# Later post-mixes, conversions moved between stages, q loaded once, other relayouts at the start of a fused attention and expert kernel

## The chip, the cores and the metric

The kernel runs on one core of a Trainium2 chip. The metric is device time in microseconds (us) of one execution. Before the change three runs took 1535.59, 1542.51 and 1545.74 us, median 1542.51. The profile is of a further execution, which took 1539.95 us.

## The reference

Three layers follow each other, in float32 (the weights of the last layer come as float64 and are converted on the chip):

```python
# attention with head mixing before and after the softmax: batch 4, heads 12, seq 448, head_dim 64
scores = scale * q @ k.T                                # per batch and head
scores = einsum('bhij,hg->bgij', scores, w_pre)         # "pre-mix" over the heads
attn   = exp(scores - max) / (sum + 1e-9)
attn   = einsum('bhij,hg->bgij', attn, w_post)          # "post-mix"
x      = (attn @ v) as [1792 tokens, 768]
# experts: 8 of them, each token goes to one (argmax of x @ w_gate), 768 -> 1024 -> 768
y[mask] = gate * (relu(x[mask] @ w1[e]) @ w2[e])
# last layer for all tokens: 768 -> 2048 -> 768
h = relu(y @ w_in); out = (h * h) @ w_out
```

## The kernel before, in words

**Prologue and attention (to about 650 us).** Each batch's 448 query rows are cut into four chunks (120, 110, 120, 98 rows; 16 chunks), and each chunk into groups of 10 rows, 180 groups in all. For a chunk, `qk` makes the scores of a head for all its rows on TensorE, ScalarE puts them into `raw`, and SP stores two heads at a time in a DRAM scratch `scr`. For a group, `pump` loads a tile `r` whose partitions are (row, head), so that `premix` is one matrix product with a block-diagonal matrix. `rmax` and `exp` give the tile `e` and its row sums; `wscale` makes their reciprocals on VectorE for two groups, `wmul` scales the post-mix matrix on GpSimd (`wr`), `postmix` multiplies `e` with `wr`, `a_hi` and `a_lo` split the result in two parts (a rounded part and the rest, as all operands of the products in float32r are split), and `av` multiplies two chunks at a time (a pair, 23 or 22 groups) with v.

The order is written out by hand. A loop runs over slots `t` from -10 to the end; slot `t` holds the pre-mix of group `t`, and a dictionary `plan` says in which slot `postmix`, `av`, `xout`, `qk`, `q_load`, `q_trans`, the loads and splits of k and v go. `LAG` is the number of slots by which the post-mixes follow the pre-mixes (from the second pair on; `L0` is that of the first pair); the last `AVS` slots of a pair hold `av` and no post-mix. All engines and DMA queues take their instructions in the order in which they are issued here, and an instruction that waits holds back those behind it on its engine.

The first chunk is special. Its q and all k of the first batch are loaded whole into `qa` and `ka`, its scores stay in SBUF as `raw0`, and its first three groups are relayouted straight from `raw0` (rows `g0` to `g0+10`, which are ten neighbouring partitions), the others through `scr`. q lies twice side by side (`z` in 0, 1), by two loads. `warm` issues products on zeros, whose results are not used.

`tick` is called three times in a slot. It hands out steps of the router (which sorts tokens to experts) and of `convert`: `w_in` and `w_out` come as float64 and each half (128 rows x 384 columns) is turned into float32 by seven VectorE steps (`Conv.parts`, lines 916 to 924) and stored in DRAM (`wi`, `wo`). Of 64 halves, 36 are converted during the attention.

**Experts (to about 1045 us).** `Moe.run` walks through units of 128 tokens, in pairs of a double unit (two units together, `double1`, `double2`) and a single one (`stage1`, `stage2`). Weights stream in, and every tile is split by ScalarE (line 1044) and VectorE or GpSimd (line 1045). The remaining 28 halves of `w_out` are converted here: after each step of a double unit (from the second one on) `CD` says how many conversion steps follow on VectorE.

**Last layer (to the end).** For four blocks of tokens and 16 slices of the 2048 columns: `st1` (line 1266), `relu2` (1276 to 1279), `st2` (1296, 1298). The converted weights are loaded from `wi` and `wo` and split again (`split_in`, `split_out`; the latter's rest is formed on GpSimd).

## Time and profile before

| what | value |
|---|---|
| median of three runs | 1542.51 us (1535.59 to 1545.74) |
| the profiled execution | 1539.95 us, its span 1538.2 us |
| TensorE (PE) busy | 1407.9 us, 92% of the span |
| TensorE weight loads (PEld) busy | 1203.7 us, 78% |
| VectorE (DVE) busy | 1035.6 us, 67% |
| ScalarE (ACT) busy | 825.1 us, 54% |
| GpSimd (POOL) busy | 466.3 us, 30% |
| moved by DMA | 279.25 MB, mean 182 GB/s |

An engine's busy time is the sum of the spans of its instructions; waiting doesn't count. Matrix products are pipelined and their ends are modelled, so a busy TensorE isn't a TensorE at its peak. The granted clock (PEclk) is a share of full speed. The name to the right of an arrow in a wait is the instruction that ended it.

### The profile page before, as it was taken

The page shows a single profiled execution, that of the slowest core. Times are in us where ns is not written, and L with a number is a line of the kernel's source. Part 1 is how long each engine was busy: PE and PEld are TensorE (multiplying, and loading weights), DVE is VectorE, ACT ScalarE, POOL GpSimd, SP SyncE. Part 2 cuts the span into 40 slices and gives each one's busy share as a digit, 9 for nine tenths or more (in the row PEclk, how much of TensorE's full clock was granted, in tenths as well). Part 3 has the DMA queues.
Part 4 walks back from the last instruction along what each step waited for, and adds up shares of the span by engine and source line. Part 5 has one row for each costly group of instructions (what it writes and reads, how often), then busy time and mean ns, then how long its engine had stood idle before and what let it go on. Part 6 is the DMA issues. An engine that isn't in the chain of part 4 may idle for free.

```text
span 1538.2 us, 25510 instructions
## 1 busy us (share of the span) xinstructions
PE 1407.9 (92%) x8541; PEld 1203.7 (78%) x8541; DVE 1035.6 (67%) x2331; ACT 825.1 (54%) x1677; POOL 466.3 (30%) x567
## 2 busy tenths in 40 slices
PE   8579998999899999889788889999999999999996
PEld 6367876787687778789677888897888888888896
DVE  3488888888988887689789889767233332422373
ACT  3357775777687767635355455564234332433453
POOL 2034232423342332233233322223222322312253
PEclk6799999999999999999899999999999999999998
DMA  7788778877877674247988988755323423433361
GB/s 145 192 237 232 221 211 246 222 207 210 242 224 219 202 208 137 99 141 189 237 245 230 290 277 300 251 180 174 103 93 90 145 85 103 128 99 97 99 196 54
DMA packets 174459, 279.25 MB, mean 182 GB/s; under 512 B 63919, under 2 KB 119535, under 8 KB 174319
## 3 DMA queue, kind: packets, MB, share of 16 engines
q1 hardware_dynamic: 166459, 254.67, 57.3%
q10 hardware_dynamic: 4788, 10.26, 2.3%
q0 software_dynamic: 3072, 12.59, 2.3%
q8 instruction: 70, 1.15, 0.3%
q14 instruction: 70, 0.57, 0.1%
HBM read 219.60 MB, written 63.51 MB: 184 GB/s over the span
## 4 chain that ended last, share of the span: by engine, by line
PE 45%; DVE 17%; DMA 4%; issue 3%; ACT 1%; POOL 0%; DVEq 0%; SPq 0%; POOLq 0%; ACTq 0%
PE ps L1266 15%; PE psb L1296 10%; PE po L1298 4%; DVE w1l L1045 3%; DVE w2l L1045 2%; PE x L270 2%; PE psb L1124 2%; PE a L236 2%; PE s L190 2%; DMA craw<-in_moe_w_out_dram 2%; DMA r<-in_moe_w_dram 2%; PE psa L1093 1%; PE qk L165 1%; DVE sm L199 1%; DVE atl L255 1%
## 5 line engine op out<-in xcount | busy, mean ns | idle before, releaser
L1045 POOL TENSOR_TENSOR w2l<-r,w2h 128x768 fp32r<-128x768 f32 x88 | 171.0, 1944 | 465.5 <-ACT w2h L1044 449.3
L1277 DVE TENSOR_TENSOR room<-room 128x512 f32<-128x512 f32 (+1 forms) x64 | 56.5, 883 | 233.3 <-ACT room L1276 233.3
L236 PE MATMUL a<-wr,e 120*128 120x120 f32 (+1 forms) x1440 | 190.8, 280 | 24.0 <-POOL wr L227 23.2
L236 PEld LDWEIGHTS a<-wr,e 120*128 120x128 f32 (+1 forms) x1440 | 180.8, 195 | 37.1 <-POOL wr L227 29.2
L165 PE MATMUL qk<-kt,qt 128*120 128x448 f32 (+2 forms) x384 | 175.0, 541 | 20.2 <-DVE qt L107 18.4
L1266 PE MATMUL ps<-yb,w1h 128*128 128x512 f32 (+1 forms) x640 | 181.7, 369 | 0.9 <-DVE yb L1253 0.5
L190 PE MATMUL s<-r,wprebd 120*120 120x448 f32 x360 | 172.4, 561 | 9.0 <-DMA r<-scr 4.5
L1296 PE MATMUL psb<-w2h,h 128*128 128x512 f32 x448 | 170.3, 396 | 0.0
L1044 ACT CAST w2h<-r 128x768 fp32r<-128x768 f32 x160 | 132.6, 834 | 65.4 <-PE psb L1124 28.2
L1044 ACT CAST w1h<-r 128x1024 fp32r<-128x1024 f32 (+1 forms) x136 | 128.3, 947 | 70.8 <-DMA r<-in_moe_w_dram 20.9
L1276 ACT ACTIVATE room<-ps 128x512 f32<-128x512 f32 (+1 forms) x64 | 34.9, 545 | 227.7 <-PE ps L1266 227.5
L1045 DVE TENSOR_TENSOR w1l<-r,w1h 128x768 fp32r<-128x768 f32 (+1 forms) x124 | 139.1, 1133 | 25.8 <-ACT w1h L1044 23.6
L227 POOL TENSOR_SCALAR wr<-wpostbd,sm 120x120 f32<-120x120 f32 x180 | 103.8, 587 | 159.8 <-DVE sm L215 80.8
L205 ACT ACTIVATE e<-s,sm 120x448 f32<-120x448 f32 x180 | 115.0, 639 | 56.5 <-DVE sm L199 55.9
L165 PEld LDWEIGHTS qk<-kt,qt 128*120 128x120 f32 (+2 forms) x384 | 70.0, 190 | 89.1 <-issue 48.9
L199 DVE TENSOR_REDUCE sm<-s 120x1 f32<-120x448 f32 x180 | 112.4, 624 | 36.0 <-PE s L190 31.4
L250 ACT CAST ath<-a 128x480 fp32r<-128x480 f32 x180 | 101.7, 568 | 64.0 <-PE a L236 63.1
L1266 PEld LDWEIGHTS ps<-yb,w1h 128*128 128x128 f32 x640 | 111.7, 189 | 22.8 <-DVE yb L1254 1.5
L166 ACT COPY raw<-qk 120x448 f32<-120x448 f32 (+2 forms) x186 | 97.9, 531 | 41.4 <-PE qk L165 29.2
L1266 PE MATMUL ps<-yb,w1l 128*128 128x512 f32 (+1 forms) x320 | 118.2, 369 | 0.8 <-DVE w1l L1045 0.8
L1124 PE MATMUL psb<-h,w2h 128*128 128x256 f32 x576 | 111.5, 295 | 0.0
L1093 PE MATMUL psa<-room,w1h 128*128 128x256 f32 x576 | 107.4, 288 | 0.0
(321 smaller groups left out, 3241.0 us busy)
## 6 DMA issues: line engine op xcount, KB each, us to landing
r<-in_moe_w_dram SPq DMA_DIRECT2D x72, 512.0 KB
r<-in_moe_w_dram SPq DMA_DIRECT2D x96, 384.0 KB
r<-scr SPq DMA_DIRECT2D x173, 210.0 KB
r<-wi SPq DMA_DIRECT2D x64, 384.0 KB
r<-wo SPq DMA_DIRECT2D x64, 384.0 KB
scr<-raw SPq DMA_DIRECT2D x48, 420.0 KB
craw<-in_moe_w_in_dram SPq DMA_DIRECT2D x32, 384.0 KB
craw<-in_moe_w_out_dram ACTq DMA_DIRECT2D x26, 384.0 KB
```

The costliest lines, as they stand in the source:

```text
L165: nc.tensor.matmul(ps[0:n], lhsT=qts[C, h // 2][:, z, h % 2, 0:n], rhs=kts[b, h], start=z == 0, stop=z == 1)
L190: nc.tensor.matmul(ps[0:m], lhsT=const["wpre"][0:m, 0:m], rhs=rts.pop(G)[0:m], start=True, stop=True)
L199: nc.vector.reduce_max(sms[G // 2][0:m, o:o + 1], pss[G][0:m], axis=AX.X, negate=True)
L205: nc.scalar.activation(t[0:m], pss.pop(G)[0:m], AF.Exp, bias=sm[0:m, o:o + 1], accum_out=sm[0:m, 2 + o:3 + o])
L227: nc.gpsimd.tensor_scalar(w.rearrange("p (g i) -> p g i", i=gm), src, sm[0:m, 6 + o:7 + o], None, ALU.mult)
L236: nc.tensor.matmul(o, lhsT=e[0:m, JT[jc]:JT[jc] + JP], rhs=w, start=True, stop=True)
L1044: nc.scalar.copy(hi, raw)
L1045: (nc.gpsimd if on_pool else nc.vector).tensor_tensor(out=lo, in0=raw, in1=hi, op=ALU.subtract)
L1093: self.nc.tensor.matmul(o, lhsT=w[:, ms], rhs=x, start=k == 0 and j == 0 and m % 2 == 0, stop=k == K1 - 1 and j == 2, skip_group_check=True)
L1124: self.nc.tensor.matmul(o, lhsT=w[:, ms], rhs=x, start=k == 0 and j == 0 and m % 2 == 0, stop=k == K2 - 1 and j == 2, skip_group_check=True)
L1266: self.nc.tensor.matmul(ps[:, 0:n], lhsT=w[:, ks], rhs=x[:, 0:n], start=k == 0 and m == 0, stop=k == KD - 1 and m == 2)
L1296: self.nc.tensor.matmul(main, lhsT=x[:, ts], rhs=w[:, 0:512], start=f == 0 and m == 0, stop=f == NF - 1 and m == 2)
```

## The change

What it does, part by part:

- Post-mixes, `av` and `xout` come one slot later (`LAG` 8 to 9), with one more buffer for `e` and one less for `r`; each `wmul` is issued at the earliest three slots ahead of its post-mix instead of with its `wscale`.
- The attention converts only `w_in` (32 halves), from the 13th slot on. The experts' stage converts 18 halves of `w_out`, two or one steps at a time instead of four to two. The other 14 are converted in the first block of the last layer, in place (`conv_out`).
- q is loaded once; for the first chunk by the ACT queue and doubled by ScalarE, for the others by SP and doubled by GpSimd (`q_copy`). The loads of the constants come behind, on the ACT queue.
- The first chunk's rows lie so that the first five groups take every fifth partition of 50, and all five are relayouted straight from `raw0`; `scr` gets the rows from 50 on only.
- The loads of v of the first batch come four slots later and its splits five; three warming products follow each of the first four heads of the prologue.

```diff
-    WARM, WARM2, RB = 12, 6, 6
+    WARM, WARM2, RB = 12, 6, 5
     Q1 = {4: (0, 4), 6: (4, 8), 8: (8, 12)}
...
     r_p = pool("r", RB)
-    e_p = pool("e", 8)
+    e_p = pool("e", 9)
     wr_p = pool("wr", 6)
...
         b, i0, m = chunks[C]
-        for z in range(2):
-            nc.sync.dma_start(a[0:m, :, z], q[b, h:h + n, i0:i0 + m, :].rearrange("h p d -> p h d"))
+        src = q[b, h:h + n, i0:i0 + m, :].rearrange("h p d -> p h d")
+        k = 0 if C else RB * GI
+        for g in range(0 if C else RB):
+            nc.scalar.dma_start(a[g:k:RB, :, 0], src[g * GI:(g + 1) * GI])
+        (nc.sync if C else nc.scalar).dma_start(a[k:m, :, 0], src[k:m])
+        copies.append((a, m))
+    copies = []
+    def q_copy():
+        a, m = copies.pop(0)
+        nc.gpsimd.tensor_copy(a[0:m, :, 1], a[0:m, :, 0])
...
         if h % 2 == 1:
-            nc.sync.dma_start(scr[C][0:n, h - 1:h + 1, :], raws[C][0:n])
+            k = 0 if C else GI * RB
+            nc.sync.dma_start(scr[C][k:n, h - 1:h + 1, :], raws[C][k:n])
...
         pend.extend(range(first[C], first[C + 1]))
-        pump(RB if C else 3)
+        pump()
...
             t = r_p.tile([GP, S], F32, tag="r", name="r")
-            if G < 3:
-                nc.sync.dma_start(t[0:m * H], raw0[g0:g0 + m])
+            if G < RB:
+                nc.sync.dma_start(t[0:m * H], raw0[G:GI * RB:RB])
             else:
...
         sm, o = sms[G // 2], G % 2
-        if o == 1:
-            sms.pop(G // 2)
         w = wr_p.tile([GP, H, GI], F32, tag="wr", name="wr")
...
-    plan = {}
+    plan, scale = {}, {}
...
     AVS, LEAD, L0 = 5, 4, 4
-    LAG = AVS + 3
+    LAG = AVS + 4
     for P in range(len(pairs)):
...
             g = LAG if P else L0
-            at(f + g + s * (w + LAG - g) // n, postmix, f + s)
+            t = f + g + s * (w + LAG - g) // n
+            at(t, postmix, f + s)
+            scale.setdefault(max((f + s) // 2 * 2 + 3, t - 3), []).append(f + s)
         for z in range(6):
...
         if g % 2 == 0:
-            at(3 * g // 2, v_load, 0, g)
-        at(3 * g // 2 + 2, v_split, 0, g)
+            at(3 * g // 2 + 4, v_load, 0, g)
+        at(3 * g // 2 + 7, v_split, 0, g)
     for C in range(NC_):
...
                     at(f + u * n // 6 - 8, q_load, C + 1, u)
+                if u % 2 == 0:
+                    at(f + u * n // 6 - 3, q_copy)
                 at(f + u * n // 6 - 2, q_trans, C + 1, u)
...
-    q_all(0, 0, 4)
+    q_all(0, 0, H)
     k_all(0, 2)
     k_all(2, 6)
-    q_all(0, 4, H)
     k_all(6, H)
...
         kns[0, h] = ka[:, h]
+    nc.scalar.copy(qa[0][:, :, 1], qa[0][:, :, 0])
+    copies.clear()
     warm(WARM)
...
             q_all(1, *Q1[h])
+        if h < AH + 2:
+            warm(3)
     fill_const(0)
...
             wscale((t - 3) // 2)
-            wmul(t - 3)
-            wmul(t - 2)
+        for G in scale.get(t, ()):
+            wmul(G)
         tick(ps_q, 0, busy, t - NG)
...
 CR = 3
-NP = 18
-FF = 1024
+FF, F2 = 1024, 2048
+K1, K2, NF = KD, FF // 128, F2 // 128
 TS = 2
...
 XK = ((4,6),(3,5))
-CD = (4,4,4,4,4,4),(4,4,4,4,3,2,2,2)
+CD = (2,2,2,2,2,2),(2,2,2,2,2,2,1,1)
 PH = (3,4,5,6,7,8,9,9,10,12,13)
...
 ZS = (12,14,16,18,20,22)
-F2 = 2048
-K1, K2, NF = KD, FF // 128, F2 // 128
 PE, END = "PE", "END"
...
         self.ph, self.py = {}, {}
-        self.todo = [(g >= NF, g % NF, z) for g in range(NP, 2 * NF) for z in range(2)] if self.main else []
+        self.todo = [(1, f, z) for f in range(NF) for z in range(2) if z == 0 or f < 2] if self.main else []
         self.loads = list(self.todo)
...
         for kind, f, z in self.todo:
-            if z == 0:
-                cw = self.cw_p.tile([128, DM], F32, tag="cw", name="cw")
             a = self.cv_p.tile([128, 384], I32, tag="ca", name="ca")
             r = self.cv_p.tile([128, 384], F32, tag="cr", name="cr")
-            yield from cv.parts((kind, f, z), cw[:, z * 384:(z + 1) * 384], a, r)
+            cw = self.cw_p.tile([128, 384], F32, tag="cw", name="cw")
+            yield from cv.parts((kind, f, z), cw, a, r)
             self.conv_load(self.nc.scalar)
-            if z == 1:
-                self.nc.sync.dma_start(cv.wo[f * 128:(f + 1) * 128] if kind else cv.wi[f], cw)
+            self.nc.sync.dma_start(cv.wo[f * 128:(f + 1) * 128, z * 384:(z + 1) * 384], cw)
...
         f = self.seq[i][1]
-        self.nc.sync.dma_start(self.raw2[i % K2], self.cv.wo[f * 128:(f + 1) * 128, :])
+        n = 384 if self.main and 2 <= i < NF else DM
+        self.nc.sync.dma_start(self.raw2[i % K2][:, 0:n], self.cv.wo[f * 128:(f + 1) * 128, 0:n])
+    def conv_out(self, i):
+        cv = self.cv
+        a, r = self.froom("h").bitcast(I32)[:, 0:384], self.froom("l")[:, 0:384]
+        out = self.raw2[i % K2][:, 384:DM]
+        for _ in cv.parts((1, i, 1), out, a, r):
+            yield
+        self.nc.sync.dma_start(cv.wo[i * 128:(i + 1) * 128, 384:DM], out)
+        if i + 4 < NF:
+            self.conv_out_load(i + 4)
+    def conv_out_load(self, i):
+        self.cv.load((1, i, 1), self.raw1[2 + i % 4][:, 0:DM].bitcast(I32), self.nc.sync)
...
-    def relu2(self, i):
+    def relu2(self, i, conv):
         nc = self.nc
...
         nc.vector.tensor_tensor(out=g[:, 0:n], in0=g[:, 0:n], in1=g[:, 0:n], op=ALU.mult)
+        next(conv, None)
         nc.scalar.copy(hi[:, 0:n], g[:, 0:n])
...
                     assert False
+            conv = self.conv_out(i + 2) if main and i + 2 < NF else iter(())
             if i < N:
-                self.relu2(i)
+                self.relu2(i, conv)
+            for _ in conv:
+                pass
             if i < N and self.seq[i][1] == NF - 1 and self.seq[i][0] + 1 < len(blocks):
...
         self.yb_p = self.pool("yb", 1)
+        if self.main:
+            for i in range(2, 6):
+                self.conv_out_load(i)
...
             const = emit_ident(tc, c0, c1)
-            load_consts(tc, c1, const, w_pre, w_post, w_gate)
             cx_p = c1.enter_context(tc.tile_pool(name="cx", bufs=2))
...
-                keys = [(g >= NF, g % NF, z) for g in range(NP) for z in range(2)]
+                keys = [(0, f, z) for f in range(NF) for z in range(2)]
...
                 for i, key in enumerate(keys):
-                    kind, f, z = key
+                    _, f, z = key
                     a, r = [xs_p.tile([128, DM // 2], F32, tag=f"c{n}", name="cx") for n in range(2)]
...
                             zs = slice(z * 384, (z + 1) * 384)
-                            nc.sync.dma_start((cv.wo[f * 128:(f + 1) * 128] if kind else cv.wi[f])[:, zs], r)
+                            nc.sync.dma_start(cv.wi[f, :, zs], r)
                             load(i + 2)
...
                     steps[:] = route(new), None
-                    next(conv)
                 if last:
                     cur[1] += 1
-                    for _ in range(1 if busy and cur[1] % 2 else 2):
+                    for _ in range(0 if cur[1] < 13 else 2 if cur[1] % 3 == 0 or not busy else 1):
                         next(conv, None)
...
                 if part:
+                    load_consts(tc, c1, const, w_pre, w_post, w_gate)
                     rt.fill()
```

## Rows read from the trace of the kernel before

**Rows 1.** Busy us (count) by stretch: PE, PEld, DVE, ACT, POOL, PEclk, DMA, GB/s.

```profile
10.00:34.00 24.00, 24.00 (x79) 20.09 (x78) 10.95 (x29) 9.82 (x21) 5.08 (x13) 0.50 0.69 154
...
34.00:51.00 17.00, 0.93 (x4) 0.31 (x2) 3.46 (x9) 0.34 (x1) 0.00 (x0) 0.60 0.45 110
...
60.00:110.00 50.00, 37.55 (x188) 27.69 (x187) 35.63 (x98) 26.42 (x65) 15.23 (x24) 0.86 0.86 239
...
110.00:600.00 490.00, 459.75 (x2930) 373.53 (x2929) 412.88 (x1238) 363.31 (x939) 170.45 (x268) 0.99 0.76 216
...
704.00:977.00 273.00, 233.01 (x1615) 217.09 (x1614) 244.10 (x367) 138.23 (x179) 85.35 (x68) 0.94 0.86 252
...
1054.00:1187.00 133.00, 132.78 (x657) 110.96 (x657) 44.75 (x63) 45.60 (x70) 28.14 (x15) 0.99 0.33 95
```

**Rows 2.** Timeline of the prologue: start us, us, engine, line, operation, out<-in, count.

```profile
0.83 1.40 ACTq L455 DMA_DIRECT2D wprerep<-in_w_pre_dram  x1
...
2.18 4.79 PE L350 MATMUL warm<-wz 120*120 120x448 f32 x12 [2.18 <-DVE wz L345]
...
3.08 0.50 ACTq L457 DMA_DIRECT2D idwg<-in_moe_w_gate_dram  x1
...
7.21 0.36 ACT L98 CAST qt<-qtp 128x240 fp32r<-128x240 f32 x1 [2.31 <-PE qtp L96]
...
17.53 1.10 PE L165 MATMUL qk<-kt,qt 128*120 128x448 f32 x2
...
21.77 1.10 PE L165 MATMUL qk<-kt,qt 128*120 128x448 f32 x2
```

**Rows 3.** Timeline behind the prologue; in brackets the idle time before, and its releaser.

```profile
32.82 4.34 SPq L182 DMA_DIRECT2D r<-raw  x3
...
37.21 3.12 SPq L170 DMA_DIRECT2D scr<-raw  x1
...
40.38 2.50 SPq L904 DMA_DIRECT2D craw<-in_moe_w_in_dram  x2
...
47.36 0.36 DVE L916 TENSOR_SCALAR cx<-craw 128x384 int32<-128x384 int32 x1 [13.40 <-DMA craw<-in_moe_w_in_dram]
...
51.17 0.71 PE L165 MATMUL qk<-kt,qt 128*110 128x448 f32 x1 [15.81 <-DVE qt L107]
...
54.70 0.92 PE L190 MATMUL s<-r,wprebd 120*120 120x448 f32 x2
...
64.74 1.82 PE L190 MATMUL s<-r,wprebd 120*120 120x448 f32 x2 [4.51 <-DMA r<-scr]
```

**Rows 4.** TensorE's waits, 60 to 600 us: us in total, times, longest.

```profile
PE a L236 <- POOL wr L227: 20.9, 19, 3.5
```

**Rows 5.** TensorE's waits, 75 to 110 us.

```profile
PE a L236 <- POOL wr L227: 7.2, 3, 3.5
```

**Rows 6.** VectorE's groups, 704 to 977 us: count, busy us, mean ns, idle before.

```profile
L917 DVE SCALAR_TENSOR_TENSOR ca<-craw,ca 128x384 int32<-128x384 int32 x28 | 20.0, 713 | 0.6
...
L916 DVE TENSOR_SCALAR ca<-craw 128x384 int32<-128x384 int32 x28 | 16.1, 576 | 13.8 <-DMA craw<-in_moe_w_out_dram 13.8
...
L918 DVE TENSOR_SCALAR craw<-craw 128x384 int32<-128x384 int32 x28 | 13.1, 469 | 0.8
```

**Rows 7.** TensorE's timeline where the second double unit starts.

```profile
704.14 0.40 PE L1093 MATMUL psa<-room,w1h 128*128 128x256 f32 x2
```

**Rows 8.** Chain that ended last, from 976 us: start us, us, what.

```profile
976.89 9.86 PE psa L1093 x72
...
1023.63 8.19 PE psa L1152 x36
...
1031.82 4.23 PE psa L1184 x24
```

**Rows 9.** The same chain in the last layer.

```profile
1076.15 4.18 PE ps L1266 x18
...
1084.57 4.18 PE ps L1266 x18
```

## Prediction

> **What bounds the kernel now.** I read the busy time by stage first [rows 1], then the stretches whose TensorE share is low, in order of time, and last what TensorE waited for. Four things are to be seen. From 10 to 34 us TensorE is recorded busy all the time, but at a granted clock of 0.50. From 34 to 51 us it is idle but for 0.93 us. In the attention (110 to 600 us) it is busy 459.75 of 490 us, so at most 30 us are to be had there. In the first expert stage (704 to 977 us) it is busy 233 of 273 us while VectorE is busy 244 and the DMA engines 0.86, so VectorE and the transfers set that stage. In the last stage (1054 us on) TensorE is busy 132.78 of 133 us and VectorE only 44.75: nothing is to be gained there, and VectorE has room.
>
> **The dead stretch after the prologue.** TensorE waits 15.81 us for `qt` from VectorE [rows 3]. VectorE does nothing either: its next instruction in order is the first conversion step, which waits 13.40 us for `craw`, and `q_lo`, which makes `qt`, is queued behind it. `craw` is late because SP first issues three `r<-raw` (4.34 us) and the last `scr<-raw` (3.12 us) and gets to `craw` at 40.38. The change starts no conversion before the 13th slot, so this wait is gone. Late next is the transfer for the first pre-mix. TensorE stood still from 51.17 - 15.81 = 35.4 us, and from its restart to the first pre-mix it needed 54.70 - 51.17 = 3.5 us: ready at 38.9. The five direct relayouts begin on SP where the three did, at 32.8; at a third of 4.34, 1.45 us, for each, the first is issued by 34.3. No row shows its landing. Nearest is `craw`: asked for at 40.38, used at 47.36, so 7 us or less. By that, 32.8 + 7 = 39.8. I take the pre-mix at 40: gain 54.7 - 40 = 14.7; ends: 3 (the transfers now take VectorE's place until 51) and 15.8.
>
> The fourth pre-mix waits 4.51 us for its `r<-scr` [rows 3]: groups 3 and 4 now come straight from `raw0`, and the group after them is asked for right behind the first pre-mix, five pre-mixes ahead of its use. Gain 4.5; lower end 0, should the sixth group wait instead. The post-mixes wait 7.2 us for `wr` between 75 and 110 us [rows 5], where VectorE has conversions and the splits of v in front of `wscale`. Both come later; the slot of each post-mix hardly moves in the first pair. I take 2 of 7.2.
>
> **The prologue itself.** q is now loaded by ACT's queue, whole, and doubled by one ScalarE copy; the constants' three DMA issues come behind that copy. They occupied ACT from 0.83 to 3.58, that is 2.75 us [rows 2], while nothing waited; now they stand ahead of the first `qt` cast, which began at 7.21. The copy (768 columns; ScalarE's 240-column cast takes 0.36 [rows 2]) waits for all twelve heads instead of four. SP is free for k in return. I take 3 us later; ends 0 and 6. The 12 more warming products cost 0.40 us each by the 12 that are there (4.79 us) [rows 2], 4.8 in all; nine of them stand ahead of or right behind the first transpose, where TensorE waits for that copy, so they are inside the 3 us. Halving q's bytes and GpSimd's copies I cost at nothing: GpSimd is busy 170 of 490 us at 0.64 us each [rows 1], some 45 copies at that mean make 29 us more, and each is asked for five slots behind its load. If that cover fails, the copy holds `wr` behind it on GpSimd, the wait of the next part.
>
> In the prologue two heads take 21.77 - 17.53 = 4.24 us [rows 2], TensorE being occupied throughout at the lower of its two levels, 1.2 GHz. I take no gain in clock: 12 products in a row are there already, and it stood at 0.50 from 10 to 34 us all the same. The Trainium skill, "TensorE: Matmul & The Clock Gate", section "Part 1: The HAM clock gate", has it that throttled is the default and that sustained activity releases it; by that more warming products would bring the upper level early, and the sum would be some 9 us better. The trace agrees in part only: recorded busy at 24 of 24 us did not bring it.
>
> Start: 14.7 + 4.5 + 2 - 3 = **18 us gained** (ends 0 and 30).
>
> **Attention.** Post-mixes of the later pairs come one slot later, and each `wr` product at most three slots ahead of its post-mix. TensorE waited 20.9 us for `wr` from 60 to 600 us [rows 4], so 20.9 - 7.2 = 13.7 behind 110 us. Today a post-mix falls, towards the end of each pair, on the slot of its `wscale` or the next; one slot more is about 3 us, near the longest of these waits (3.5). But VectorE is busy 412.88 of 490, and what is late next is its `sm` chain for the exponentials. I take **8**; ends 0 and 15. The conversions' density hardly changes: 32 halves of seven steps begin 13 slots later, instead of 36. One slot is added to the tail, and its products leave the slots before: nothing. One `r` buffer less: a group is still asked for five slots ahead, at some 3 us a slot (180 groups from 54.70 to a little over 600), so 15 us, against at most 64.74 - 54.70 = 10 us for the fourth group's, which was asked for behind the first pre-mix: nothing; without that cover each us of lateness at the 15 later chunks' starts costs 15.
>
> **The first expert stage.** Before, the four pairs of units (a double one and a single one) beside which conversions run, 49 steps to a pair, 196 in all for 28 halves, go from 704.14 to 976.89 [rows 7, 8]: 68.2 us a pair. The fifth has none: its two first layers and the double second layer take 1023.63 - 976.89 = 46.7, and a single second layer is twice 4.23: 55.2 us a pair where TensorE alone sets the time. A step of a conversion costs VectorE between 469 and 713 ns [rows 6], the seven groups together 118.6 us for 196 steps: 0.605 each. After, there are 18 halves, 126 steps, 26 to each of five pairs. VectorE's demand per pair falls from 244 / 4 = 61 by 23 x 0.605 = 13.9 to 47, under TensorE's 55. Transfers: 252 GB/s x 273 us / 4 = 17.2 MB a pair [rows 1]; seven halves (393 kB in, 197 kB out each) make way for 3.7, which leaves 15.3 MB, at the same rate 60.6 us. So the DMA engines come last, at 60 us a pair: 5 x 60 = 300 against 272.8 + 55.2 = 328. **Gain 28**; ends: 52 (all five at 55.2) and 8 (64 us a pair).
>
> **The last stage.** 14 halves, 98 steps, go into the first 14 steps of the block from 1054 us, seven each. A step lasts 1084.57 - 1076.15 = 8.4 us [rows 9]; VectorE is busy 44.75 / 133 x 8.4 = 2.8 of it, plus 4.24 at most: 7.0. `relu2`'s subtraction has only one conversion step before it, and its product is used a whole step later. The loads are asked for four steps (33 us) ahead. Cost 0; what covers it is the 1.4 us left on VectorE. Uncovered, it costs what is over: GpSimd's subtraction is 28.14 us for the stage's 15, 1.9 each [rows 1]; were VectorE shut out for that long in each step, it would need 8.9, and 14 steps give 14 x 0.5 = 7 us. The Trainium skill, "SBUF — State Buffer", section "Who interferes with whom", speaks for that: a VectorE instruction with two SBUF inputs and a GpSimd one that reads SBUF shut each other out. In this trace the two-input step is at 713 ns in the expert stage; whether that is GpSimd's doing no row shows.
>
> **Sum.** 18 + 8 + 28 = 54. The profiled execution took 1539.95, 2.6 us below the median of 1542.51: 1486 of it, and **1488** against the median.
>
> **Rivals.**
> - TensorE alone sets the expert stage (gain 52 instead of 28): 1464. For: the last pair, at 55.2. Against: the DMA share of 0.86. Chance 0.14.
> - The clock is held high through the prologue: five double heads from 4.24 to about half, less what ScalarE and VectorE need: 9 us, 1479. For it 12 more products; against it the 0.50. Chance 0.09.
> - Transfers keep setting the expert stage (gain 8): 1508. For: `craw` made VectorE wait 13.8 us there [rows 6], and the bytes per us hardly fall. Against: VectorE's 13.9 us a pair. Chance 0.13.
> - The dead stretch only changes its owner, and TensorE waits for the relayouts (start gains 3): 1503. Against: three of them were through SP by 37.2. Chance 0.06.
> - GpSimd and VectorE shut each other out in the last stage: 1495. Chance 0.05.
> - The later post-mixes don't lift the `wr` wait, since VectorE, not the slot, is late; the change then does not do what it says there: 1496. Chance 0.04.
> - Slower: in the first block of the last stage, VectorE waits in order for a conversion's load, with the next subtraction and the next split queued behind it. It waited 13.40 for such a load once [rows 3]. To lose, each of 14 steps must grow by more than 54 / 14 = 3.9 us; at 5 the time is 1558. It decides only if loads land over 33 us after issue, against 7 above. Chance 0.04.
> - Both of the transfer cases together, relayouts and experts: 1523 to 1530, no change that can be told. Chance 0.06.
>
> The forecast keeps 0.39, with 1472 to 1502 of its own. The range runs from 1458 to 1514: it leaves out the slower case, the double one and the outer tails. About 1% (15 us) is what a measurement of this kernel can tell from no change. Faster, below 1527: all but the last two, 0.90; within: 0.06; slower: 0.04.
>
> **What would show it.** Right: no TensorE wait for `qt` before the first pre-mix, which starts near 40 us; `wr` waits below 12 us in all; the five pairs near 60 us each; steps of 8.4 us in the last stage up to its 14th. Wrong: the first pre-mix behind 48 us, pairs above 65, or a wait for `h` from VectorE in the last stage.

## The result and the profile after

The changed kernel took 1504.53 us (median of four runs, 1503.69 to 1505.51), the kernel before, on the same chip, 1541.99: ratio 0.9761, interval 0.9728 to 0.9795. It is faster by 37 us; 1488 was forecast, inside a range of 1458 to 1514. The profiled execution took 1505.51, its span 1503.5, 34.7 less than before.

Cut at four places that both traces have, the two spans say where it came from: VectorE's row maximum (`rmax`) of the 9th pre-mix (84.90 us before, 77.67 after), the place where the chain of work that ended last enters the second double unit (704.14, 708.58; its first product, to 0.2 us), one and the same product in the first step of the last layer (1054.33, 1019.35), and the end.

| stretch | before | after | gained | forecast |
|---|---|---|---|---|
| start to the 9th pre-mix | 84.9 | 77.7 | +7.2 | +18 |
| from there to the second double unit | 619.2 | 630.9 | -11.7 | +8 |
| from there to the last layer | 350.2 | 310.8 | +39.4 | +28 |
| last layer | 483.9 | 484.1 | -0.2 | 0 |

So the experts' stage gave more than the whole gain, the attention lost what the start had won, and more. The busy time by stage (columns as in [rows 1]; the last two lines are the stretches that answer to the last two there):

```profile
10.00:34.00 24.00, 18.16 (x60) 15.44 (x61) 6.68 (x19) 9.14 (x17) 2.18 (x3) 0.54 0.25 46
34.00:51.00 17.00, 16.30 (x56) 12.36 (x55) 6.47 (x21) 7.08 (x17) 3.95 (x12) 0.64 0.35 99
60.00:110.00 50.00, 43.98 (x223) 32.62 (x222) 39.37 (x107) 31.20 (x80) 18.16 (x30) 0.90 0.82 237
110.00:600.00 490.00, 449.69 (x2847) 362.74 (x2847) 403.43 (x1204) 354.25 (x912) 183.51 (x298) 0.99 0.69 201
708.00:943.00 235.00, 225.47 (x1616) 212.79 (x1616) 193.11 (x277) 136.22 (x178) 90.79 (x68) 0.97 0.94 264
1019.00:1152.00 133.00, 132.77 (x658) 111.22 (x658) 106.47 (x161) 45.78 (x70) 29.95 (x15) 0.99 0.42 135
```

The stretch that was dead, 34 to 51 us, is busy, but with the prologue's own work: the clock is still low there for the most part (0.64). In the attention TensorE is busy 449.69 of 490 us, ten less than before. In the experts' stage it went from 85% to 96% busy, with the DMA engines at 0.94.

**The start.** The timeline of the changed kernel's prologue, which answers to [rows 2]:

```profile
0.84 4.75 ACTq L86 DMA_DIRECT2D qa<-in_q_dram  x5
...
2.19 5.35 PE L364 MATMUL warm<-wz 120*120 120x448 f32 x18 [2.19 <-DVE wz L359]
...
6.07 0.39 ACTq L87 DMA_DIRECT2D qa<-in_q_dram  x1
...
13.62 1.28 ACT L386 ACT_TABLE_LOAD   x1 [13.62 <-DMA qa<-in_q_dram]
...
14.91 0.83 ACT L386 COPY qa<-qa 120x768 f32<-120x768 f32 x1
...
15.84 0.63 PE L107 MATMUL qtp<-ident,qa 120*128 120x120 f32 x2 [8.31 <-DMA wprerep<-in_w_pre_dram]
...
19.59 1.10 PE L176 MATMUL qk<-kt,qt 128*120 128x448 f32 x2
```

The five loads that spread the rows over every fifth partition take ACT's queue 4.75 us to issue. The last part of q is asked for at 6.07, while k's loads run, and is there at 13.6. The copy waits for all of it, and so the first `qk` starts at 19.59 instead of 8.92. Between the landing and the copy stands ScalarE's table load, 1.28 us; in the kernel before it ran at 3.62, while nothing waited for it. TensorE's wait is put down to `wprerep`, but its line says when it ended (15.84), and the copy's end at 15.74 is what it waited for. Then, behind the prologue (answers to [rows 3]):

```profile
44.48 5.92 SPq L194 DMA_DIRECT2D r<-raw  x5
...
49.86 0.92 PE L202 MATMUL s<-r,wprebd 120*120 120x448 f32 x2
...
50.44 2.76 SPq L182 DMA_DIRECT2D scr<-raw  x3
...
57.69 0.53 ACT L177 COPY raw<-qk 110x448 f32<-110x448 f32 x1 [7.02 <-DMA scr<-raw]
...
59.14 1.85 PE L202 MATMUL s<-r,wprebd 120*120 120x448 f32 x2 [6.59 <-ACT e L217]
```

The wait for `qt` (15.81 us) is gone. Three stores of the second chunk's scores come behind five relayouts on SP. Until they land, no `raw` buffer is free; ScalarE waits 7.02 us with its copy of `raw`, the exponentials stand behind it in order, and the third pre-mix stands 6.59 us for `e`. By the fourth pre-mix (61.90, against 64.74) 2.8 us of the gain are left.

**The attention.** TensorE's waits from 60 to 640 us (total, times, longest):

```profile
PE qtp L107 <- POOL qn L94: 24.7, 19, 2.4
PE s L202 <- ACT e L217: 9.7, 10, 6.6
```

The waits for `wr` ([rows 4]; 23.2 us to 640) are all gone. In their place TensorE waits 24.7 us for GpSimd's copies of q.

**The experts.** VectorE's conversion steps from 704 to 977 us (answers to [rows 6]), and the chain of waits where the fourth and fifth pair start ([rows 8]):

```profile
L932 DVE SCALAR_TENSOR_TENSOR ca<-craw,ca 128x384 int32<-128x384 int32 x18 | 10.0, 554 | 0.3
...
L931 DVE TENSOR_SCALAR ca<-craw 128x384 int32<-128x384 int32 x18 | 9.2, 513 | 0.0
L933 DVE TENSOR_SCALAR craw<-craw 128x384 int32<-128x384 int32 x18 | 8.2, 453 | 0.3
```

```profile
708.58 11.52 PE psa L1108 x96
...
888.47 8.64 PE psa L1108 x72
...
943.13 8.64 PE psa L1108 x72
```

18 steps of each kind instead of 28, and the 13.8 us of waiting for `craw` are gone. What had held TensorE up there were waits for VectorE. The three longest before (704 to 977 us; idle 40.0 us in all), then the two longest after (708 to 943 us; idle 9.5 in all):

```profile
PE psa L1054 <- DVE h L1172: 14.6, 4, 9.4
PE psb L1152 <- DVE w1l L1045: 13.2, 5, 3.6
PE psa L1184 <- DVE w2l L1045: 11.9, 4, 3.0
```

```profile
PE psa L1069 <- ACT xg L1079: 2.7, 2, 2.3
PE psa L1199 <- DVE w2l L1060: 2.0, 2, 1.7
```

So 30.5 us of the four pairs' gain are waits that ended; the other 7.5 are TensorE's busy time (233.01, now 225.47, for as many products), at a granted clock of 0.97 instead of 0.94. Four pairs take 943.13 - 708.58 = 234.6 us, 58.6 a pair (68.2 before); the last of them, 888.47 to 943.13, 54.7, about the 55.2 of the pair without conversions.

**The last layer** keeps its step ([rows 9]). The chain of waits there:

```profile
1066.17 4.18 PE ps L1294 x18
...
1074.51 4.18 PE ps L1294 x18
```

8.3 us again, with conversions beside it. One thing in VectorE's groups there, and in the timeline of one step, was not expected at this size:

```profile
L936 DVE SCALAR_TENSOR_TENSOR room<-r,room 128x384 f32<-128x384 uint32 x14 | 29.2, 2084 | 0.5
...
L937 DVE TENSOR_TENSOR room<-room 128x384 f32<-128x384 f32 x14 | 7.8, 558 | 0.5
```

```profile
1049.74 2.01 POOL L1060 TENSOR_TENSOR w2l<-r,w2h 128x768 fp32r<-128x768 f32 x1 [5.28 <-ACT w2h L1059]
...
1050.08 2.09 DVE L936 SCALAR_TENSOR_TENSOR room<-r,room 128x384 f32<-128x384 uint32 x1
```

This conversion step takes 2084 ns each of 14 times, where the same step takes 555 in the attention and the experts' stage. Each time it starts some 0.3 us behind the start of GpSimd's subtraction and ends some 0.4 us behind its end.

The kernel before had the same in its experts' stage, and not for steps with two inputs alone. Of its conversion steps there 17 took 1.0 to 2.6 us, each begun under a subtraction of GpSimd and ended 0.2 to 0.4 us behind it. Eleven of them have a single input, like this one (`cr<-ca`, median 353 ns):

```profile
902.16 1.84 POOL L1045 TENSOR_TENSOR w2l<-r,w2h 128x768 fp32r<-128x768 f32 x1 [1.82 <-ACT w2h L1044]
902.45 1.77 DVE L919 TENSOR_SCALAR cr<-ca 128x384 int32<-128x384 int32 x1
```

The step whose mean of 713 ns the prediction left open is among them too: three of its 28 are in the 17, and the other 25 average 555 ns. So that mean was GpSimd's doing.

### The profile page after: what moved, and what is told of

Its sections match the earlier page's. It is cut to its first block, busy times and chain, and to the rows that moved or that the text cites. A ratio compares the mean times of both kernels' runs of the same rounds, so it can differ in the third digit from the quotient of the medians.

```text
span 1503.5 us, 25533 instructions
## 1 busy us (share of the span) xinstructions
PE 1403.9 (93%) x8553; PEld 1199.5 (80%) x8553; DVE 1048.1 (70%) x2331; ACT 824.8 (55%) x1678; POOL 496.0 (33%) x612
## 4 chain that ended last, share of the span: by engine, by line
PE 65%; DVE 16%; DMA 9%; issue 4%; SPq 2%; ACT 2%; POOL 1%; DVEq 0%; POOLq 0%; ACTq 0%
PE ps L1294 15%; PE psb L1325 10%; PE psb L1139 5%; PE psa L1108 5%; PE po L1327 4%; PE a L246 4%; PE x L280 4%; PE s L202 4%; PE qk L176 3%; DVE sm L211 3%; DMA r<-in_moe_w_dram 3%; DVE atl L265 3%; PE psa L1199 2%; DMA scr<-raw 2%; DMA craw<-in_moe_w_out_dram 2%
## 5 line engine op out<-in xcount | busy, mean ns | idle before, releaser
L1060 DVE TENSOR_TENSOR w1l<-r,w1h 128x768 fp32r<-128x768 f32 (+1 forms) x124 | 144.1, 1173 | 22.9 <-ACT w1h L1059 21.4
L237 POOL TENSOR_SCALAR wr<-wpostbd,sm 120x120 f32<-120x120 f32 x180 | 107.5, 606 | 146.9 <-DVE sm L227 90.8
L1327 PE MATMUL po<-w2h,h 128*128 128x256 f32 x384 | 107.2, 279 | 0.0
```

The lines of the kernel that those rows point to most:

```text
L237: nc.gpsimd.tensor_scalar(w.rearrange("p (g i) -> p g i", i=gm), src, sm[0:m, 6 + o:7 + o], None, ALU.mult)
L1060: (nc.gpsimd if on_pool else nc.vector).tensor_tensor(out=lo, in0=raw, in1=hi, op=ALU.subtract)
L1327: self.nc.tensor.matmul(rest, lhsT=x[:, ts], rhs=w[:, 512:768], start=f == 0 and m == 0 and t % 2 == 0, stop=f == NF - 1 and m == 2, skip_ ...
```

## Experiments

Twelve more kernels were run. The kernel before took 1542.02 us beside E1 to E4, 1544.93 beside E5 to E8 and 1547.38 beside E9 to E12, so ratios are compared, not times. "Attention" is the second stretch of the table above, "9th" the end of the first, both from one profiled execution of each kernel. The clock is that granted from 10 to 34 us (0.50 is the lower level, 1.2 GHz, 1.00 the upper, 2.4 GHz).

| kernel | median | ratio to before | 9th | attention | clock |
|---|---|---|---|---|---|
| before | 1541.99 | | 84.9 | 619.2 | 0.50 |
| changed | 1504.53 | 0.9761 (0.9728 to 0.9795) | 77.7 | 630.9 | 0.54 |
| E1 copy earlier | 1494.89 | 0.9683 (0.9665 to 0.9700) | 78.8 | 620.2 | 0.56 |
| E2 q loaded twice | 1500.43 | 0.9738 (0.9703 to 0.9774) | 77.1 | 622.6 | 0.51 |
| E3 first q as before | 1491.40 | 0.9658 (0.9640 to 0.9677) | 62.5 | 634.0 | 0.93 |
| E4 conversions alone | 1497.38 | 0.9712 (0.9693 to 0.9731) | 80.3 | 617.6 | 0.72 |
| E5 E4, begun late | 1503.68 | 0.9721 (0.9671 to 0.9772) | 72.7 | 629.3 | |
| E6 E4, later post-mixes | 1509.09 | 0.9726 (0.9657 to 0.9796) | 82.9 | 623.9 | 0.50 |
| E7 E1 and E3 together | 1485.66 | 0.9612 (0.9548 to 0.9677) | 63.9 | 621.6 | 1.00 |
| E8 E7, old warming | 1495.27 | 0.9668 (0.9619 to 0.9717) | 71.3 | 624.8 | 0.52 |
| E9 changed, old warming | 1509.30 | 0.9755 (0.9733 to 0.9777) | 76.3 | 633.2 | 0.50 |
| E10 E4, new warming | 1492.64 | 0.9651 (0.9635 to 0.9667) | 76.5 | 617.5 | 0.95 |
| E11 E7, old post-mixes | 1496.16 | 0.9667 (0.9651 to 0.9683) | 67.0 | 624.3 | 0.95 |
| E12 E7, q loaded twice | 1485.18 | 0.9606 (0.9584 to 0.9628) | 62.3 | 622.3 | 1.00 |

**E1, the copy of q two slots earlier** (changed kernel).

```diff
-                    at(f + u * n // 6 - 3, q_copy)
+                    at(f + u * n // 6 - 5, q_copy)
```

> The changed kernel with GpSimd's copies of q two slots earlier in its order (five slots ahead of the chunk's place instead of three); nothing else. Theory A (the copy stands behind wr and v work that waits for VectorE on GpSimd's queue, one slot ahead of the transpose that needs it): TensorE's 24.7 us of waits for the copy fall below 5, and the time falls by 12 to 20 us, to about 1488. Rival (VectorE sets the attention, and any wait that goes is replaced by another): below 4 us of gain, 1501 to 1505.

Its waits from 60 to 640 us begin so; the one for the copy is gone:

```profile
PE s L202 <- ACT e L217: 16.0, 17, 7.4
PE a L246 <- DVE ath L267: 4.0, 4, 2.7
PE a L246 <- POOL wr L237: 3.7, 3, 2.3
```

Against the changed kernel the ratio falls by 0.0078, 12 us; the attention is 10.7 us shorter. The copy's place was the fault: half of the 24.7 us come back, the rest goes into other waits, above all those for `e` (16.0 us, 9.7 in the changed kernel) and `wr`.

**E2, q of the later chunks loaded twice, no copy** (changed kernel).

```diff
-        (nc.sync if C else nc.scalar).dma_start(a[k:m, :, 0], src[k:m])
-        copies.append((a, m))
+        for z in range(2 if C else 1):
+            (nc.sync if C else nc.scalar).dma_start(a[k:m, :, z], src[k:m])
```

> The changed kernel with q of all chunks but the first loaded twice by SP, as before, and no copy on GpSimd. Theory A: the wait for the copy is gone altogether, 15 to 20 us faster, about 1487, for 21 thousand more packets of 256 bytes. Rival (VectorE sets the attention): 1501 to 1505. Second rival (the halved loads of q helped the transfers by as much): 1500 or slower.

The attention is 8.3 us shorter too, but the runs spread from 1493.19 to 1506.83 and the interval overlaps the changed kernel's; by itself this decides nothing. E12 repeats it on a better base.

**E3, the first chunk's q as before** (changed kernel; two loads by SP, four heads first, rows in order; the five direct relayouts stay).

```diff
+        if C == 0:
+            for z in range(2):
+                nc.sync.dma_start(a[0:m, :, z], src)
+            return
...
-                nc.sync.dma_start(t[0:m * H], raw0[G:GI * RB:RB])
+                nc.sync.dma_start(t[0:m * H], raw0[g0:g0 + m])
...
-    nc.scalar.copy(qa[0][:, :, 1], qa[0][:, :, 0])
```

> The changed kernel with the first chunk's q as before: loaded twice by SP, four heads first, rows in neighbouring partitions, no ScalarE copy; the five direct relayouts remain, from ten neighbouring partitions each. Theory B (the first chunk's q lands at 13.6 us because its last load stands behind k, and the whole prologue starts 10.7 us later): first score product near 9 us instead of 19.6, time 9 to 11 us less, about 1494. Rival (the relayouts from neighbouring partitions take longer and give it back): first pre-mix at 45 or later, gain below 4.

The first `qk` starts at 10.2 us, the clock is at its upper level, and the first pre-mix comes at 30.8 instead of 49.9. 15 us of it are left at the 9th, and 16 in the ratio (0.0103), more than the 9 to 11 of the theory, which had not counted on the clock. With ten neighbouring partitions each, the five relayouts took SP 8.76 us to issue (spread: 5.92), and the third pre-mix waited 9.67 us.

**E4, the conversions alone** (kernel before with only the conversions moved; the early ones keep their first step and pace).

```diff
-CD = (4,4,4,4,4,4),(4,4,4,4,3,2,2,2)
+CD = (2,2,2,2,2,2),(2,2,2,2,2,2,1,1)
...
-                keys = [(g >= NF, g % NF, z) for g in range(NP) for z in range(2)]
+                keys = [(0, f, z) for f in range(NF) for z in range(2)]
```

> The kernel before with the moved conversions alone: w_in in the attention at the old pace, 18 halves in the expert stage, 14 in the last layer's first block. Theory C (the whole gain comes from the expert stage, 38 us): 1542 - 38 = 1504, the same as the changed kernel within 4 us. Rival (start and attention gained too, the expert stage less): 1515 or more.

This part alone gives 0.9712: 7.6 us more than the whole change, better than both theories had it (the two intervals just touch). So the rest of the change gained nothing that shows, and probably had a price.

**E5, E4 with the conversions begun at the 13th slot.**

```diff
-                    next(conv)
...
-                    for _ in range(1 if busy and cur[1] % 2 else 2):
+                    for _ in range(0 if cur[1] < 13 else 2 if cur[1] % 3 == 0 or not busy else 1):
```

> The kernel before with the moved conversions (as in the run that had them alone, 1497) and the late first conversion (13th slot, two steps in every third slot): no other part. Theory of the prediction (the dead stretch is the in-order wait for the first conversion's load, 15.8 us): TensorE's wait for qt goes, first pre-mix near 40 us instead of 52, 8 to 15 us faster, about 1486. Rival D (SP's relayouts and the store of raw scores behind them take the place of that wait, as in the changed kernel at 52 to 59 us): gain below 4, 1494 to 1499.

The first pre-mix starts at 39.25, where the prediction had put it (40), but no gain over E4 is to be seen in the time (the interval leaves room for some 6 us at most). Two things stand against it. The third pre-mix (timeline of E5) waits for `e`, as in the changed kernel:

```profile
39.25 1.01 PE L190 MATMUL s<-r,wprebd 120*120 120x448 f32 x2
...
50.04 1.85 PE L190 MATMUL s<-r,wprebd 120*120 120x448 f32 x2 [6.45 <-ACT e L205]
```

And the conversions end later. The fourth step of E4's halves in the attention, then E5's (count, durations in ns, first and last start in us):

```profile
L919 DVE SCALAR_TENSOR_TENSOR cx<-craw,cx x32: 536/558/896, 46.4 to 481.6; 128x384 f32<-128x384 uint32 x32
```

```profile
L919 DVE SCALAR_TENSOR_TENSOR cx<-craw,cx x32: 548/559/900, 67.6 to 554.9; 128x384 f32<-128x384 uint32 x32
```

E5 is 7.6 us ahead of E4 at the 9th pre-mix, and takes 11.7 us more from there to the second double unit. From the 101st pre-mix to the last, 242.0 us became 254.9. From 480 to 560 us, where E4 (first line) is through with its conversions but for the last half and E5 (second) is not, TensorE is busy 6 us less in E5 (columns as in [rows 1]):

```profile
480.00:560.00 80.00, 78.69 (x514) 64.53 (x512) 62.96 (x199) 61.58 (x160) 26.21 (x43) 1.00 0.69 193
```

```profile
480.00:560.00 80.00, 72.72 (x469) 58.39 (x467) 69.28 (x212) 57.05 (x149) 24.36 (x38) 1.00 0.73 209
```

Conversions that leave the start come back at the attention's end. That rests on one execution of each, and that nothing else took part isn't shown.

**E6, E4 with the later post-mixes** (`LAG` 9, nine `e`, five `r`, `wmul` by `scale`).

```diff
-    LAG = AVS + 3
+    LAG = AVS + 4
...
+            scale.setdefault(max((f + s) // 2 * 2 + 3, t - 3), []).append(f + s)
```

> The kernel before with the moved conversions and the later post-mixes alone (slot, wr product at most three slots ahead, one buffer more for e, one less for r). Theory of the prediction: the waits for wr (20 us in the run with the moved conversions alone) go, 8 us faster, about 1489. Rival E (TensorE and VectorE are both near their bound in the attention, 23 us of idle in 490, so a wait that goes is used up by smaller ones): 1494 to 1500.

The waits for `wr` (20.4 us in E4) are gone, waits for `e` (11.1 us, 3.0 in E4), `qt` and `ath` grew, and no gain is to be seen; but the runs spread from 1495.99 to 1513.51, and the interval would hold the 8 us that were forecast.

**E7, E1 and E3 together, with three relayouts ahead of the stores.**

```diff
-        pump()
+        pump(RB if C else 3)
```

> The changed kernel with the first chunk's q as before, GpSimd's copies two slots earlier, and three relayouts first, the fourth and fifth behind the first pre-mix. Theory A and B together: from 1504.5 less 10 for the copies, less 13 for q, less up to 6 for the stall on SP between the first pre-mixes: 1476 to 1482. Rival D (the stores of raw scores stay behind the relayouts): the third pre-mix still waits over 6 us, and the time stays at 1482 to 1488.

The third pre-mix still waits for `e`, 5.10 us instead of 9.67 in E3:

```profile
40.50 1.85 PE L204 MATMUL s<-r,wprebd 120*120 120x448 f32 x2 [5.10 <-ACT e L219]
```

The time is where the rival had it (1482 to 1488), the wait is shorter than it said, and the interval, the widest but one here, holds both theories. Against the changed kernel the ratio falls by 0.0149; E1 and E3 apart give 0.0078 and 0.0103. So what the order of relayouts and stores adds is not shown.

**E8, E7 without the twelve additional warming products.**

```diff
-        if h < AH + 2:
-            warm(3)
```

> The same as the run before it, without the twelve additional warming products. Theory F (with q there early, they keep TensorE at the upper level through the prologue, where two heads take 2.4 us instead of 4.24): the granted clock from 12 to 28 us is 0.50, the first pre-mix comes 7 to 9 us later, the time is 4 to 9 us longer. Rival (the clock is up because the prologue is denser, not for the products): 1.00 there as well, same time within 2 us.

From 10 to 34 us, E7 and then E8 (columns as in [rows 1]):

```profile
10.00:34.00 24.00, 20.07 (x104) 15.12 (x103) 13.45 (x39) 12.70 (x29) 6.62 (x16) 1.00 0.61 134
```

```profile
10.00:34.00 24.00, 23.96 (x81) 20.05 (x79) 11.11 (x30) 9.83 (x22) 5.94 (x15) 0.52 0.44 101
```

The products hold the clock: the median `qk` product from 14 to 32 us takes 454 ns with them, 575 without, the first pre-mix starts at 31.03 against 38.43, and 8.6 us (0.0056) of it reach the end, though the two intervals overlap.

**E9, the changed kernel without them** (the same edit).

> The changed kernel without the twelve additional warming products. Theory A (there the products buy nothing, because q lands at 13.5 us and the granted clock is 0.50 from 10 to 34 us with them too): same time as the changed kernel, 1500 to 1508 us, first pre-mix at 49 to 51 us. Theory B (they are worth in any order of loads what they were worth with q early, 1495.3 against 1485.7 us): 1511 to 1517 us, first pre-mix about 8 us later.

Ratio 0.9755 against 0.9761: with q late they do nothing that shows. TensorE stands still in front of the first transpose for 8.31 us with them and 9.55 without, and the clock is down afterwards either way (0.54, 0.50).

**E10, E4 with them** (the same lines added).

> The kernel before with the conversions moved (1497.4 us) and the twelve warming products, nothing else. Theory A (the products hold the clock whenever q comes early, and nothing later eats the gain): the two-head period goes from 4.2 to about 2.4 us, the first pre-mix comes 7 to 10 us earlier, and the time is 1488 to 1491 us. Theory B (the relayouts, stores and waits behind the first pre-mixes end at their own time, as with the late first conversion, where a first pre-mix at 39.2 us gave nothing): first pre-mix earlier, first expert product as with the conversions alone (649.8 us), time 1495 to 1499 us.

By the ratio the time is as the first theory has it (9.4 us better than E4, intervals apart). The first pre-mix at 47.34 is not; it comes 4.9 us earlier than E4's instead of 7 to 10: E4's profiled execution had the upper level in part (0.72), and the stretch for `qt` is as long as ever:

```profile
39.90 0.36 DVE L916 TENSOR_SCALAR cx<-craw 128x384 int32<-128x384 int32 x1 [13.43 <-DMA craw<-in_moe_w_in_dram]
...
43.71 0.71 PE L165 MATMUL qk<-kt,qt 128*110 128x448 f32 x1 [16.79 <-DVE qt L107]
```

**E11, E7 with the post-mixes of before** (`LAG` 8, eight `e`, six `r`, `wmul` no earlier limit).

```diff
-    LAG = AVS + 4
+    LAG = AVS + 3
...
-            scale.setdefault(max((f + s) // 2 * 2 + 3, t - 3), []).append(f + s)
+            scale.setdefault((f + s) // 2 * 2 + 3, []).append(f + s)
```

> The best kernel so far (changed kernel with the first chunk's q as before, the copy two slots earlier and three relayouts first, 1485.7 us) with the post-mixes and their scaling at their slots of before (lag 8, six r, eight e). Theory A (the later post-mixes only exchange waits: wr 23.2 us gone, others come): 1483 to 1489 us, with 15 to 25 us of waits for wr back in the trace and the waits for e smaller. Theory B (they are worth the waits that they take away, with the copy's wait now gone too): 1495 to 1505 us.

The `wr` wait is back:

```profile
PE a L248 <- POOL wr L239: 28.1, 21, 3.7
```

The ratio is 0.0055 above E7's, but E7's interval holds it, and the attention differs by only 2.7 us. Neither theory is shown.

**E12, E7 with q loaded twice** (the edit of E2).

> The best kernel so far with the later chunks' q loaded twice as before, so that GpSimd has no copy at all. Theory A (the copy five slots ahead is already covered, so only transfers are added): 1485 to 1491 us. Theory B (the copy still costs, as its wait in GpSimd's queue or as the waits of e and qt behind it): 1476 to 1483 us.

No difference to E7 (0.9606, 0.9612): three slots ahead of its transpose instead of one, the copy is covered. These two are the fastest kernels here, 0.015 (23 us) below the changed one, both with their intervals apart from its.

## Why the prediction came out as it did

The forecast was faster by 54 us against the profiled execution; 34.4 came. The sign rests on the experts' stage, as said; the terms of the start and of the attention failed, and that stage's surplus covers part of the miss. With its 28 us as forecast instead of 39.4, the time would have been 1516, outside the range: that it lies inside is partly luck. Of the prediction's own signs, those for `wr`, the pairs and the last layer's steps came out right; the first pre-mix, at 49.86, came behind the 48 us that were to show it wrong.

- **Experts, +28, measured +39.4.** That VectorE's conversions held TensorE up was right: of 40.0 us of waits 9.5 are left, and E4, which moves the conversions alone, gains 38.3 us in the same stretch. The size was off in two places. 15.3 MB a pair was right (264 GB/s x 234.6 us / 4 = 15.5), but at 264 GB/s, not 252: 58.6 us a pair instead of 60. And the sum put the fifth pair at 60 as well, where it had stood at 55.2 before and gained 1.2 (from 77.4 us to the last layer to 76.2). That the transfers come last now, as the sum had it, is not shown: the DMA engines are at 0.94, but TensorE is 96% busy, and its waits are 2.4 us a pair. The clock's share, some 7.5 us in the four pairs, was in no term.
- **The prologue, 3 us later, measured 10.7.** The failing step is the sentence that counted the q load as the issues of three constants and a copy. The six issues on one queue and the landing at 13.6, behind k's, were not costed, nor the table load of 1.28 us in front of the copy. E3 takes it back as a whole: 16 us with the clock that goes with it. What each part cost was not tried apart.
- **The dead stretch, +14.7.** Its cause was right: with the late conversion the wait for `qt` is gone and the pre-mix stands at 39.25 (E5). But the rival that it only changes its owner is what the time showed, in two steps that were not named there: the stores behind the relayouts on SP, which hold ScalarE's copy and with it `e`, and the conversions' end, which moves from 481.6 in E4 to 554.9 in E5 (and from 533.3 in the kernel before to 571.1 in the changed one). "The conversions' density hardly changes" was the failing sentence: it looked at how dense they are and not at where they end. E5 takes 11.7 us more than E4 in the attention; by how much the later end alone is the cause is not shown.
- **The clock, no gain taken.** Right for the kernel as it was changed (E9), wrong as a reason: that 12 products at the start had not kept it up didn't show that more between the heads would not. In E7, E10 and E12 they do (1.00, 0.95 and 1.00), and the rival's 9 us are what E8 and E10 measure (8.6 and 9.4). Without them the level is low in most of the profiled executions, but not in all (E4: 0.72). The Trainium skill, "TensorE: Matmul & The Clock Gate", section "Part 1: The HAM clock gate", has it that sustained activity releases the throttle; E7 against E8 agrees with that, and the bare record "busy 24 of 24 us at 0.50" was the weaker witness.
- **GpSimd's copies, cost nothing.** This failed: 24.7 us of waits, 10.7 us of time (E1). The cover named, five slots from the load to the copy, was the wrong one: what was short is the one slot from the copy to the transpose. The consequence named, `wr` held up, did not come; `qtp` was.
- **Later post-mixes, +8.** The `wr` waits fell to 0, further than the 12 us that the prediction asked for. But waits for `e` took their place: E6 shows no gain, E11 can't tell 8 us from none, and the worth of this part stays open.
- **Last layer, 0.** Right: waits of 0.9 us in all. The rival's mechanism was there, though: 14 x (2084 - 555) = 21 us more on VectorE, covered by its free time (busy 106.47 of 133 us). The cost per step, 1.5 us, is within the 1.9 that the rival gave it. The Trainium skill, "SBUF — State Buffer", section "Who interferes with whom", has it that an instruction with two SBUF inputs contends with GpSimd's reads; the 14 steps agree. Two inputs are not needed for it, though: in the kernel before eleven steps with one input were held up as long.

## What to carry to other kernels

An idle stretch at the start of a pipeline is worth taking away only if the work that filled it, or was served in it, isn't moved to where engines are full: look where the moved work now ends, not only where it began. When a step is put between a load and its reader, on an engine that takes its work in order, leave slots in front of the reader too, not only behind the load: one slot cost 24.7 us of waits here, three covered it (E7 against E12). Cost a transfer that every later step waits for by the landing of its last part, not by its issues alone: a copy that needs the whole of it waits for that part.

## What the runs showed of the hardware

- A relayout's issue took longer from neighbouring partitions: five took SP 5.92 us from spread ones (5.72 to 5.92 in the changed kernel, E1, E2 and E9), and 8.76 us from neighbouring ones in E3.
- The recorded clock was wrong for a whole stretch once. E5's window from 10 to 34 us says 1.00, and its `qk` products from 14 to 32 us last as long as those of kernels at 0.50. Two heads take 4.24 us there as in the kernel before, and 2.4 in E7, which is at 1.00 too. E5's lines:

```profile
10.00:34.00 24.00, 24.00 (x78) 20.15 (x79) 10.27 (x27) 10.34 (x22) 5.05 (x13) 1.00 0.70 154
```

```profile
L165 PE MATMUL qk<-kt,qt x19: 575/575/727, 14.1 to 32.0; 128*120 128x448 f32 x19
```

That is why its clock is left out of the table.
- VectorE's step with two inputs, begun 0.3 us into GpSimd's subtraction, stretched from 555 to 2084 ns in 14 of 14 cases of the last layer. In the kernel before, steps with one input did so too: 1.77 instead of 0.35 us in the line above.
